# A new order table for the steps of a fused linear-attention and gated-MLP kernel

## The chip, the cores and the metric

The kernel runs on one core of a Trainium2 chip. The metric is the device time of one execution in microseconds (us). TensorE is called PE in the profile (its weight loads PEld), VectorE DVE, ScalarE ACT, GpSimd POOL and SyncE SP. Every load and store of data, but one small one that POOL issues, is issued from SP's queue.

## The reference, cut to what matters

There are 4 batches, 8 heads, 768 time steps and 48 columns per head, in float32. The first part is a gated linear recurrence with one 48 by 48 state per batch and head; its output, heads side by side, is the input x (768 by 384) of a gated MLP with a spatial mix.

```
for t in range(S):
    state = alpha[:, :, t, :, None] * state + einsum('bhd,bhe->bhde', k[:, :, t], v[:, :, t])
    y[:, :, t] = einsum('bhd,bhde->bhe', q[:, :, t], state)
...
h = maximum(x @ w_in, 0)                  # 384 -> 1024
u, v = h[..., :512], h[..., 512:]
v_n = (v - mean(v)) / sqrt(var(v) + 1e-6)
v_s = einsum('ts,bsd->btd', w_spatial, v_n) + b_spatial[None, :, None]
out = (u * v_s) @ w_out                   # 512 -> 384
```

## The kernel before

**Stages.** Time is cut into chunks of 128 steps: 6 chunks per batch, 24 in all, numbered 0 to 23. The first 8 chunks are worked in 4 *pairs* (0 to 3) of 256 steps, the others singly. The work is cut into 1156 *steps*, each bound to one engine. A step's name is used below with the number of its pair or chunk.

- Loads: `ac`, `kc`, `qc`, `vc` bring alpha, k, q and v; a pair's load is 384 KB, a chunk's 192 KB. They are numbered by chunk, so pair 1 is `ac 2` and so on. `w_in 1` and `w_in 0` are the two column halves of w_in, `w_sp 0` to `w_sp 2` thirds of w_spatial, and `w_out` the last weight. Weights land in a float32 buffer (`raw_w`, two of them) and are cast to bf16 (`cast`).
- Attention of a pair: `lnp` takes the log of alpha on ACT; `cump` sums it over time by a matmul with a triangle of ones (built on POOL by `c_tri`); `einvp` and `eexpp` take exp of minus and plus that sum (ACT); `ktp` and `qtp` scale k and q by them; `vbp` casts v; `tr k` and `tr q` transpose on PE and `ev` copies the result from PSUM; `sc` computes scores; `m` masks them (DVE); `ya` and `y` make the output from scores and from the state. `updq`, `z`, `S`, `ebcp` and `sb` update the state, scale it, and copy it for the next `y`.
- Attention of a single chunk: the same, as `ln`, `cum`, `einv`, `eexp`, `kt`, `qt`, `vb`, `trk`, `ev`, `upd`, `sc`, `m`, `y`.
- `xs` casts an output to bf16, `xt` transposes it, `xe` copies it into x transposed.
- The MLP of batch b: `v b t` is x @ w_in's second half with a ReLU; `bn`, `rs`, `vn` normalise it (mean and variance, reciprocal root, scaling); `u b f h` is the first half; `wt` and `we` transpose w_spatial; `s b d h` is the spatial matmul in two parts and an addition of the bias on DVE; `g` multiplies by u (POOL or DVE); `o b t` is the product with w_out and its copy from PSUM, and `st` the store. The last output tile is made in two half-column pieces, `oh`. `bb` and `be` spread the bias.
- `c_...` steps fill constants at the start; `c_junk` fills the operand of junk matmuls.

**Order.** Nothing is ordered while the program runs but by semaphores. The Python code first lists all steps with what each depends on, and `replay` then emits them in the order of the table `PLAN` (lines 57 to 108). A word of the table is a letter for the engine (P for PE, D for DVE, A for ACT, G for POOL, S for an issue on SP, Q for the landing, which emits nothing) and the step's number. So the table sets each engine's own sequence, and with it which of the allowed engines does a step. Each engine runs its sequence strictly as emitted. `P58:512:512:192` adds junk: before the step's first matmul, PE runs float32 matmuls of 512, 512 and 192 columns into that step's PSUM bank. PSUM's 8 banks go round in the order in which `bank()` is called, so also in the table's order.

Of the kernel before, what the change touches and what calls it, by code (L numbers as in the profile page):

```python
# [60 lines left out]
P134:512:108 P86 G121 D122 A135 P78 D87 S182 Q183 P126 D88 P124 P89 D80 S184 Q185 A186 P136 D91 A79 A127 D90 G81 A137  # L61
G123 D83 A125 G82 P149:512:500 A133 S322 Q323 P146 D151 P92 A22 D150 P96 A93 P197 D23 A97 D21 P94 D147 P187 A198 P98
A95 S24 Q25 D148 G200 A188 P100:228 A189 G190 P203 S326 Q327 A199 P138 D191 A101 D201 G84 A99 P195 D102 G8 A204 P205
G85 P193 A139 P103 D140 S324 Q325 A202 D206 G141 D196 P152 A104 D143 G142 A194 P215 S29 Q30 D105 G192 P153 A330 P157
G144 P207 D154 A106 G145 D158 P155 P331 D209 A156 D216 P341 A208 P159 G28 A332 D217 P212 A160 G210 A26 D214 P172 G211
A342 D213 P161 A333 G27 A173 D335 P218 S33 Q34 A343 A162 S328 Q329 P219 D345 P170 G334 A220 S382 Q383 D163 P223 P349
P221 A224 S384 Q385 P164 G344 D350 A222 P339 D174 A171 P225 P337 A165 P168 D340 A226 P166 D107 A175 D338 P227 A167
D176 D108 A169 P230 D32 A228 D177 P238 A231 D31 P247 S386 Q387 D35 A239 P347 D232 A248 P250 P244 A249 P242 G36 D229
A348 P236 A252 D251 P362 A233 S37 Q38 G346 D245 P253 D246 A243 G336 P240 D364 A237 S424 Q425 P351 A390 D363 A255 S428
Q429 D235 P359 A254 D234 P391 A352 D353 S388 Q389 P274 D360 A393 A241 G354 P270 A392 D356 P275 D361 A395 G394 P266  # L70
D276 P267 G357 D396 P271 A40 G39 D268 P398 D272 P259 S426 Q427 G355 A400 P365 D399 A261 D260 P256 G358 P405 S430 Q431
D366 A432 P369 P278 G269 D370 S495 Q496 P367 P433 D258 A368 P371 G273 D257 P279 S41 Q42 D407 A372 P294 A434 G397 D406
P295 A435 S461 Q462 G277 A437 D280 P376 S463 Q464 G436 P408 D296 P282 D438 A409 G439 P401 A377 P290 D402 A503 S465
Q466 P410 P440 G403 D411 P283 D412 A441 G281 D442 P373 D284 G297 P291 A374 P420 D292 S499 Q500 G285 A46 P447 D421 P443
P504 S497 Q498 A469 G43 D378 P413 A45 G404 P470 A44 S592 Q593 D449 P286 A472 A505 D448 P416 S467 Q468 A471 P287 D444
A474 D417 P418 G445 S501 Q502 A507 D288 P306 G473 A414 D508 S594 Q595 A419 P450 D415 G293 A307 P422 A451 S596 Q597
P298 D475 A423 G506 D375 S663 Q664 P477 A299 P452 G476 P302 A479 D453 D478 G289 A600 P480 P510 A303 D481 P484 S626
Q627 G446 D454 A512 P601 D511 P318 D485 G482 A602 S598 Q599 A603 A379 D486 P513 G483 P314 A605 S665 Q666 D515 G604
A319 P487 A509 D606 S628 Q629 P455 A488 D514 P608 S705 Q706 A456 D315 P489 P516 A610 D609 P310 S632 Q633 G607 D490
A517 D457 A491 P615 A671 P518 S630 Q631 P492 D519 A520 D381 A458 P521 D311 A493 D617 P530 A522 S667 Q668 D616 P528  # L80
A494 P611 D380 P534 S707 Q708 A529 D460 A634 P532 D459 D612 A523 S743 Q744 P548 G613 A531 P672 D524 P635 G641 S777
Q778 A713 P540 D533 A535 P618 A525 S709 Q710 P560 A674 A637 A636 D527 P544 D526 S669 Q670 A673 G638 P714 A639 P561
A676 S711 Q712 D640 P549 G614 A619 D677 P541 A715 S779 Q780 G675 D550 A716 P545 A751 D542 P642 S781 Q782 G551 P620
D562 P552 A622 D621 A718 S749 Q750 P553 D546 G543 A643 D719 P645 P623 A644 S745 Q746 D554 G717 A785 D646 P649 A678
P679 S747 Q748 G647 D650 P721 A624 P556 G547 A723 D651 P557 A681 D722 G563 P652 D680 S783 Q784 P682 D558 A653 P686
G555 P728 D683 S877 Q878 P654 D687 P536 A656 G684 A655 P537 D688 A720 S873 Q874 G648 P786 D729 P752 A787 P564 S907
Q908 G685 D538 A754 A758 P724 P657 D730 A753 S875 Q876 G539 A789 P565 D725 A658 D790 S990 Q991 P731 G755 A756 D566
P689 A732 P568 D757 G788 A690 D659 P759 A569 P733 S879 Q880 G726 P691 P576 D734 A692 G559 D625 A735 A760 S909 Q910
# [1071 lines left out]
```

## Time and profile before

| | |
|---|---|
| median of 3 runs | 142.24 us (142.18 to 142.88) |
| profiled execution | 142.43 us, of which the span of instructions is 140.6 us |
| granted TensorE clock, mean | 0.997 |
| busy PE / DVE / ACT / POOL | 135.3 / 118.5 / 108.1 / 83.9 us |
| DMA | 28.64 MB in 89000 packets, mean 204 GB/s |
| junk matmuls | 22 instructions, 10.7 us |

Busy time of PE has modelled ends and can overlap waits, so the gaps from start to start of its steps are read as well. A line of the timeline gives start, duration, engine, line of the code, operation and tiles; lines of helpers (`copy` is L198 on ACT and L200 elsewhere, matmuls of the MLP are all L819) are told apart by tiles. Of idle time, the brackets name what ended it.

### The profile page before, as it was taken

What the parts mean: (1) busy time and instruction counts of PE and PEld (TensorE: products, weight loads), DVE (VectorE), ACT (ScalarE), POOL (GpSimd) and SP (SyncE); (2) the same over time, 40 slices, a digit from 0 to 9 for tenths busy, and PEclk for the clock granted to TensorE, in tenths of its full rate; (3) what the DMA queues carried; (4) which work ended last, traced back from release to release, by engine and by line L of the source; (5) the groups of instructions that cost most, each with busy time, mean ns of one, the idle gap of its engine ahead of it and who ended that gap; (6) DMA issues with size and microseconds to landing.
All of it is one profiled execution on the core that took longest, in us unless ns stands there. A gap on an engine that the chain in (4) does not pass through costs nothing.

```text
span 140.6 us, 4974 instructions
## 1 busy us (share of the span) xinstructions
PE 135.3 (96%) x1921; PEld 84.1 (60%) x1921; DVE 118.5 (84%) x292; ACT 108.1 (77%) x279; POOL 83.9 (60%) x148
## 2 busy tenths in 40 slices
PE   7999999999999999999999999999999999999990
PEld 3357566574767656665665765656657666566560
DVE  7187799989999789899689999999899899987850
ACT  3487898899976678999989699989967978751021
POOL 6816458861469996970289999402788599002520
PEclk9999999999999999999999999999999999999998
DMA  4999997989999979989999998999999120005535
GB/s 101 320 324 328 338 254 245 295 286 315 267 226 161 306 145 215 203 175 210 188 199 190 188 200 171 199 200 220 257 222 225 71 107 7 0 23 212 215 146 192
DMA packets 89000, 28.64 MB, mean 204 GB/s; under 512 B 83728, under 2 KB 87440, under 8 KB 88976
## 3 DMA queue, kind: packets, MB, share of 16 engines
q1 hardware_dynamic: 88944, 28.32, 81.8%
q8 instruction: 15, 0.25, 0.7%
q14 instruction: 9, 0.07, 0.2%
q0 software_dynamic: 32, 0.00, 0.0%
HBM read 23.60 MB, written 4.72 MB: 201 GB/s over the span
## 4 chain that ended last, share of the span: by engine, by line
PE 59%; ACT 9%; DMA 9%; SPq 7%; POOL 5%; DVE 5%; issue 4%; ACTq 0%; POOLq 0%
PE bank L819 42%; SPq L432 7%; DMA raw_w<-in_moe_w_in_dram 5%; DMA ac<-in_alpha_dram 3%; PE bank L710 3%; PE bank L745 2%; PE bank L773 2%; PE bank L731 2%; PE bank L657 2%; PE bank L767 1%; POOL kt L681 1%; DMA out_dram<-raw_w 1%; PE bank L389 1%; POOL kt L474 1%; ACT vn L880 1%
## 5 line engine op out<-in xcount | busy, mean ns | idle before, releaser
L819 PE MATMUL bank<-w_spT,vn 128*128 128x384 bf16 x192 | 35.9, 326 | 0.0
L980 POOL TENSOR_TENSOR gT<-vsb,uT 128x384 bf16<-128x384 f32 x27 | 25.0, 939 | 12.5 <-DVE vsb L967 12.1
L819 PEld LDWEIGHTS <-vn 128*128 128x128 bf16 x192 | 17.3, 97 | 10.2
L681 POOL TENSOR_TENSOR kt<-kc,binv 128x384 bf16<-128x384 f32 x16 | 14.6, 917 | 11.9 <-ACT bc L676 7.3
L756 DVE TENSOR_TENSOR ptm<-bank,mask 128x512 bf16<-128x512 f32 x32 | 20.5, 680 | 0.7 <-PE bank L745 0.6
L819 PE MATMUL bank<-xT,w_in 128*128 128x384 bf16 x96 | 19.9, 326 | 0.0
L967 DVE TENSOR_TENSOR vsb<-bank,bsp_bc 128x384 f32<-128x384 f32 x31 | 16.6, 551 | 3.6 <-PE bank L819 3.0
L819 PE MATMUL bank<-w_in,xT 128*128 128x512 bf16 x72 | 18.8, 379 | 0.3 <-ACT xT L198 0.2
L819 PE MATMUL bank<-w_out_sb,gT 128*128 128x384 bf16 (+1 forms) x100 | 18.6, 320 | 0.0
L198 ACT COPY kqT<-bank 128x512 bf16<-128x512 bf16 x28 | 15.9, 598 | 2.2 <-PE bank L710 1.5
L335 POOL TENSOR_TENSOR state<-state,bc 128x192 f32<-128x192 f32 x20 | 10.1, 506 | 12.4 <-DVE mvs L896 5.5
L200 POOL CAST sbd<-state 64x192 bf16<-64x192 f32 x40 | 13.7, 341 | 2.1
L204 ACT ACTIVATE v_sb<-bank 128x512 bf16<-128x512 f32 x20 | 12.0, 602 | 2.4 <-PE bank L819 2.3
L884 DVE BATCH_NORM_STATS2 stats<-v_sb 128x6 f32<-128x512 bf16 x20 | 13.6, 682 | 0.0
L204 ACT ACTIVATE uT<-bank 128x384 bf16<-128x384 f32 x23 | 10.9, 492 | 2.2 <-PE bank L819 2.0
L819 PEld LDWEIGHTS <-w_in 128*128 128x128 bf16 x96 | 8.7, 97 | 5.9
L198 ACT COPY xT<-bank 128x192 bf16<-128x192 bf16 (+1 forms) x25 | 9.0, 377 | 4.1 <-PE bank L389 2.9
L819 PEld LDWEIGHTS <-gT 128*128 128x128 bf16 x100 | 8.8, 97 | 5.0
L188 PE MATMUL bank<-junk 128*128 128x512 f32 (+6 forms) x22 | 10.7, 613 | 1.1 <-DVE junk L1050 1.1
L585 DVE TENSOR_TENSOR ptm<-bank,mask 128x512 bf16<-128x512 f32 x16 | 10.3, 682 | 1.0 <-PE bank L574 1.0
L198 ACT CAST x_sb<-bank 128x384 bf16<-128x384 f32 x19 | 9.0, 494 | 2.3 <-PE bank L773 2.3
L916 DVE TENSOR_SCALAR vn<-v_sb,mvs,rstd 128x512 bf16<-128x512 bf16 x24 | 8.9, 404 | 1.5 <-ACT rstd L909 1.5
(129 smaller groups left out, 281.2 us busy)
## 6 DMA issues: line engine op xcount, KB each, us to landing
ac<-in_alpha_dram SPq DMA_DIRECT2D x16, 192.0 KB, 4.0
kc<-in_k_dram SPq DMA_DIRECT2D x16, 192.0 KB, 4.0
qc<-in_q_dram SPq DMA_DIRECT2D x16, 192.0 KB, 4.2
vc<-in_v_dram SPq DMA_DIRECT2D x16, 192.0 KB, 4.0
raw_w<-in_moe_w_spatial_dram SPq DMA_DIRECT2D x3, 768.0 KB, 5.5
out_dram<-raw_w SPq DMA_DIRECT2D x11, 192.0 KB, 2.9
out_dram<-o_sb SPq DMA_DIRECT2D x9, 192.0 KB, 1.9
ac<-in_alpha_dram SPq DMA_DIRECT2D x4, 384.0 KB, 4.6
```

What stands on the lines that cost most here:

```text
L188: nc.tensor.matmul(out=flat[:, 0:cols].rearrange("p (a b) -> p a b", a=4), lhsT=junk, rhs=junk[:, None, 0:n].to_broadcast([128, 4, n]), st ...
L198: nc.scalar.copy(out=out, in_=in_)
L200: ENG[eng].tensor_copy(out=out, in_=in_)
L204: nc.scalar.activation(out=out, in_=in_, func=AF.Relu)
L335: ENG[eng].tensor_tensor(out=st["state"], in0=st["state"], in1=st["bc"][:, :, None].to_broadcast([128, HP, D]), op=ALU.mult)
L585: nc.vector.tensor_tensor(out=st[f"ptm{par}"][:, s], in0=st[f"pt{s}{par}"], in1=mask2[:, par], op=ALU.mult)
L681: ENG[eng].tensor_mul(out=k_blocks(kt3)[:, :, :, 0:D], in0=quad(st["kc"]), in1=st["binv"])
L756: nc.vector.tensor_tensor(out=st["ptm"][:, s], in0=st[f"pt{s}"], in1=mask4, op=ALU.mult)
L819: return lambda ps: nc.tensor.matmul(out=out(ps), lhsT=lhsT(), rhs=rhs(), start=start, stop=stop)
L884: nc.vector.bn_stats(out=stats, in_=d["v_sb"][:, tt, :])
L967: nc.vector.tensor_tensor(out=hold["vs"], in0=ps[:, 0:TH], in1=bsp_bc[:, th, :], op=ALU.add)
L980: ENG[eng].tensor_tensor(out=bt[b]["gT"][:, dsl, cols], in0=hold["vs"], in1=bt[b]["uT"][:, dsl, cols], op=ALU.mult)
```

## The change

The table `PLAN` is replaced; nothing else. The table was made by a search that began with both pieces of w_in requested right behind the loads of the first pairs; the table that came out has them as the 10th and 15th issue of SP, which is where they were. All 1156 steps are there in both tables. 105 steps are given to another engine; DVE has 265 steps (260 before), ACT 253 (258), PE 300, POOL 115 and SP 111 in both. Junk columns are 5468 (4312 before).

The table's diff, first and last lines:

```
-D0 S49 Q50 D17 D13 S109 Q110 G47 Q48 D5 S53 Q54 G10 D7 S51 Q52 D2 D3 D11 G18 D15 D12 D1 S55 Q56 A57 G14 S111 Q112 G16
-P58:512:512:192 P264 A59 P68 A60 S113 Q114 G9 A69 D62 A70 D6 P66:512:232 S115 Q116 D71 P262 A67 D4 P74 A117 D61 S178
-Q179 D72 A263 P128:492 D75 A265 P118 D73 A129 P76 S19 Q20 P64 A130 G131 D65 A119 D77 S180 Q181 A120 G63 D132
...
+D0 S49 Q50 D1 D6 S51 Q52 G47 Q48 D12 D13 S109 Q110 D3 G14 D4 S53 Q54 D11 D5 G9 D15 D17 G18 S111 Q112 A57
+P68:512:512:192 S113 Q114 P264 A69 P262 P58 D263 A70 A59 S55 Q56 D2 A60 D61 G71 A265 S178 Q179 A117 D72 D62 G16
+P74:512:512:448 P118 S115 Q116 P76 P64 A119 P66 D77 A75 G121 D65 A120 S19 Q20 D7 D67 G10 P89:512:208 P128 S180 Q181
...
```

In names, each engine's sequence at the start. Junk columns stand in brackets ahead of their step.

```
SP   before: ac 0, ac 2, qc 0, kc 0, vc 0, kc 2, qc 2, vc 2, ac 4, w_in 1, kc 4, qc 4, vc 4, ac 6, w_in 0, qc 6, kc 6, w_sp 0, w_sp 1, vc 6, ac 8
SP   after:  ac 0, kc 0, ac 2, qc 0, kc 2, qc 2, vc 0, ac 4, vc 2, w_in 1, kc 4, qc 4, vc 4, ac 6, w_in 0, qc 6, kc 6, w_sp 0, w_sp 1, vc 6, ac 8
PE   before: [1216] cump 0 0, bb 1, cump 0 1, [744] tr q 0 0, bb 0, tr k 0 1, [492] cump 1 1, cump 1 0, tr q 0 1, tr k 0 0, [620] tr k 1 1, sc 0 0, updq 0, tr q 1 0, tr k 1 0, sc 0 1, tr q 1 1, [1012] sc 1 1, sc 1 0, ya 0, y 1, cump 2 1, xt 0, cump 2 0, xt 1, [228] v 0 0, tr k 2 1, updq 1, tr q 2 0, tr q 2 1, tr k 2 0, v 0 1, ya 1, sc 2 1, y 2, y 3, updq 2, xt 2, cump 3 0, cump 3 1, xt 3, sc 2 0, v 0 3, v 0 2, ya 2
PE   after:  [1216] cump 0 1, bb 1, bb 0, cump 0 0, [1472] tr k 0 1, cump 1 0, tr q 0 1, tr k 0 0, tr q 0 0, [720] sc 0 1, cump 1 1, [1024] tr q 1 0, updq 0, sc 0 0, tr q 1 1, tr k 1 0, tr k 1 1, [656] sc 1 0, ya 0, sc 1 1, y 1, cump 2 0, xt 1, xt 0, cump 2 1, updq 1, v 0 1, tr k 2 0, tr q 2 0, [260] tr q 2 1, v 0 0, tr k 2 1, ya 1, sc 2 0, y 2, y 3, updq 2, xt 2, xt 3, sc 2 1, cump 3 0, v 0 2, cump 3 1, v 0 3, ya 2
ACT  before: lnp 0, einvp 0 0, eexpp 0 0, einvp 0 1, eexpp 0 1, ev q 0 0, lnp 1, be 0, be 1, einvp 1 1, eexpp 1 1, einvp 1 0, eexpp 1 0, ev k 1 1, lnp 2, ebcp 0, ev q 1 0, ev q 1 1, ev k 1 0, vbp 1 1, cast w_in 1 1, xs 0, xs 1
ACT  after:  lnp 0, einvp 0 1, eexpp 0 1, einvp 0 0, eexpp 0 0, be 1, lnp 1, einvp 1 0, ev k 0 1, eexpp 1 0, einvp 1 1, eexpp 1 1, ebcp 0, lnp 2, ev k 1 0, ev q 1 1, cast w_in 1 0, cast w_in 1 2, cast w_in 1 1, xs 1
DVE  before: ... vbp 0 1, ev k 0 0, ev q 0 1, qtp 1 1, qtp 1 0, m 0 0 0, m 0 0 1, z 0, m 0 1 1, m 0 1 0, z 1, m 1 1 1, m 1 1 0, cast w_in 1 2, cast w_in 1 0, m 1 0 0, m 1 0 1, qtp 2 0, qtp 2 1, bn 0 0, z 2, ev q 2 1, ev q 2 0, z 3, bn 0 1, xs 2, xs 3, z 4, m 2 1 0, m 2 1 1, m 2 0 1, m 2 0 0
DVE  after:  ... ev k 0 0, c_col, ev q 0 0, m 0 1 1, m 0 1 0, qtp 1 0, ktp 1 1, qtp 1 1, ev q 1 0, z 0, m 0 0 1, m 0 0 0, ev k 1 1, z 1, m 1 0 1, xs 0, m 1 0 0, m 1 1 0, m 1 1 1, qtp 2 0, z 2, qtp 2 1, ev k 2 0, z 3, ev q 2 1, bn 0 1, ev k 2 1, bn 0 0, m 2 0 1, z 4, m 2 0 0, m 2 1 1, m 2 1 0
POOL before: b_sp, c_m4, c_m2 1, c_tri, c_m2 0, c_id, ktp 1 1, vbp 0 0, ktp 1 0, S 0, vbp 1 0, sb 0, ...
POOL after:  b_sp, c_tri, c_id, c_m2 1, ktp 0 1, c_m2 0, ktp 1 0, c_m4, vbp 0 0, vbp 0 1, vbp 1 0, vbp 1 1, S 0, sb 0, ...
```

Further on, three casts of w_spatial go from DVE to POOL (`cast w_sp 0 0`, `0 1`, `1 0`) and one from POOL to ACT. `vbp 3 1` goes from POOL to DVE. Ahead of SP's last load stand two stores (six before). The end of PE's sequence:

```
before: ... s 3 2 1 (second part), s 3 3 1 (second part), s 3 1 1 (both parts), o 3 0, o 3 2, o 3 1, oh 0, o 3 4, o 3 3, oh 1
after:  ... s 3 1 1 (both parts), s 3 3 1 (second part), o 2 5, o 3 2, o 3 0, o 3 3, oh 0, o 3 1, o 3 4, oh 1
```

More of the change, by code (lines that the diff above doesn't have):

```diff
@@ L63 @@
[L63 to L87, printed above, removed]
@@ new lines @@
+Q502 A479 G446 P480 A478 D303 P298 G506 S705 Q706 A307 D481 P283 D508 A600 G289 S598 Q599 A299 P510 D284 P484 A511
+P450 G482 D485 P601 A512 G285 P422 D486 A451 S663 Q664 P513 A603 A602 P452 G483 P487 D454 A605 S707 Q708 D514 P310
+G604 A453 A488 D606 P455 A423 S628 Q629 D515 A379 P489 P608 A311 D509 S626 Q627 P314 D609 A610 D491 P516 A456 D490
+S632 Q633 D607 P492 D380 A315 D457 A517 S669 Q670 P615 A493 P518 P318 D381 A458 D519 D520 A713 P611 D459 P521 A319
+D616 S709 Q710 A494 P532 D617 A522 S630 Q631 P530 D460 P534 A523 D533 S665 Q666 P618 A671 D612 P528 D524 A634 G613
@@ new lines @@
+P548 S777 Q778 D619 A525 G614 P635 D535 A531 P620 S667 Q668 P560 A641 D527 D621 P714 A637 A636 D526 S779 Q780 P540
+A715 G638 P549 A622 S745 Q746 A716 A529 P561 D550 G717 A639 P645 S711 Q712 A718 P541 D640 G551 P672 D562 S743 Q744
+P642 A674 A673 D646 P544 D542 A644 G647 P545 S781 Q782 D643 A676 G675 P552 D719 A678 S907 Q908 D677 P553 G648 D546
+P649 S747 Q748 P721 G563 D554 P679 P682 D650 A681 P623 G547 A722 D651 P536 A624 S873 Q874 D683 G543 P652 D680 A723
+P537 D625 S749 Q750 A653 G684 P686 A785 P728 D538 G685 P654 S948 Q949 P564 A655 D656 D687 A751 G720 P786 P657 S783
@@ L109 @@
+G1120 P1136 A870 P1128 S871 Q872 A1137 P1140 S1138 Q1139 D1129 P1148 S1130 Q1131 A1141 P1132 D1149 S1142 Q1143 P1144
+S1150 Q1151 D1133 P1152 S1134 Q1135 A1145 A1153 S1146 Q1147 S1154 Q1155
 """
```

59 lines of the change are left out of this document (36 added, 23 removed).

## The prediction

> **What bounds the kernel now.** I read the page's head first, then the timeline of the first 20 us, the landings of the DMA issues, the busy time by stretches, and the timeline of the end.
>
> ```profile
> span 140.6 us, 4974 instructions
> PE 135.3 (96%) x1921; PEld 84.1 (60%) x1921; DVE 118.5 (84%) x292; ACT 108.1 (77%) x279; POOL 83.9 (60%) x148
> ...
> PE   7999999999999999999999999999999999999990
> ...
> DMA  4999997989999979989999998999999120005535
> ...
> PE 59%; ACT 9%; DMA 9%; SPq 7%; POOL 5%; DVE 5%; issue 4%; ACTq 0%; POOLq 0%
> ```
>
> TensorE is busy in every slice, and the chain that ended last lies on it for 59%. The order of PE's own work cannot make that work shorter, so a new order can only change the time in which PE waits. The DMA engines are full up to 105 us and then empty. Where PE waits shows first in the start:
>
> ```profile
> 4.28 0.84 ACT L443 ACTIVATE la<-ac 128x768 bf16<-128x768 f32 x1 [2.26 <-DMA ac<-in_alpha_dram]
> ...
> 5.41 0.14 POOL L273 MEMSET lt_pair<- 64x64 bf16 x1
> ...
> 11.09 1.28 PE L188 MATMUL bank<-junk 128*128 128x512 f32 x4
> ...
> 14.08 0.84 ACT L443 ACTIVATE la<-ac 128x768 bf16<-128x768 f32 x1 [0.86 <-PE bank L502]
> ...
> 17.19 0.62 ACT L198 CAST w_in<-raw_w 128x512 bf16<-128x512 f32 x1 [0.34 <-DMA raw_w<-in_moe_w_in_dram]
> ```
>
> The columns are start, duration, engine, line, operation and, in brackets, idle time and what ended it. Up to 20 us PE is filled with junk matmuls while the first chain log, cumsum, exp, transposes, scores and masks runs. The landings of the DMA issues go by place in SP's queue and not by name: 4.25, 5.46, 6.67, 7.89, 9.08, 10.39, 11.61, 12.80, 13.99 us, then 17.17 for the first piece of w_in. That is 1.21 us for each 384 KB and 3.18 for a piece of w_in.
>
> **The change, part by part.** All 1156 steps stay. 105 of them change engine; DVE gets five more, ACT five fewer. Both pieces of w_in keep their places in SP's queue (10th and 15th), and the queue's places 10 to 21 are the same loads, so w_in lands at 17.17 and 26.09 as before; "right behind the first pairs' loads" is only where the search began. What changes are the loads ahead, the junk, and the engines' orders.
>
> *Start, to the 45th PE step* (`ya` of pair 2, behind the same 44 steps in both tables). Before, it starts at 28.42, just behind the last mask on DVE (27.53 to 28.21). In the new order:
> - The first log still waits for 4.25. `c_tri` now runs first on POOL (1.21 us from about 2.0) and is no longer the last to come (5.55 before); first exp 6.07 against 6.15: -0.1.
> - ACT does four exps and one bias copy (about 0.5 each) to 8.7, then the log of pair 1 to 9.5 (alpha lands at 6.67). PE has 1472 junk columns ahead of `tr k 0 1`. The 744 columns at 6.95 took 1.25 us, 1.68 ns a column, so these end at about 9.43, as that log does. The cover is full. Without it, the 1156 extra junk columns of the table would cost 1.94 us.
> - k of pair 0 lands 2.4 us sooner, q 1.2 later (7.89), needed at 8.3. The first scores start at 11.8 (12.53 before).
> - Then it loses: 1024 junk columns end at 14.2, `updq 0` comes at 14.4 (12.88 before). ACT has `ebcp 0` ahead of the log of pair 2, so that log starts at 15.4 instead of 14.08, though its alpha lands at 12.80. Behind it stand the two copies that `sc 1 0` needs (0.5 each); `sc 1 0` starts at 17.3, `y 1` at 18.4 against 17.73: +0.7.
> - From 17.8 DVE works through 8 masks (0.61 from start to start: 4.9), one `xs` (0.47), 2 `qtp` (1.0), 3 `ev` (1.0), 3 `z` (0.8), 2 `bn` (1.7), and waits 0.5, mostly for one exp: 10.4, so the last mask ends at 28.3 and `ya` starts then. Before, the same stretch ran from 17.12 and held besides two casts of w_in (0.7), two `xs` in place of one and two `ev` in place of three. These moves to ACT give the 0.7 back: -0.1.
>
> *To 42 us.* The same count brings both tables to their 65th step (again the same set) at 36.2 against 36.6. Then `updq 3` waits 0.4 for a copy of v that is now on DVE, behind `we` and `vn`: even. I take 0 for all up to 42 us; each of some ten hand-overs may be off by 0.1 to 0.2, so bounds of -0.6 and +0.7.
>
> In this stretch three casts of w_spatial go from DVE to POOL. The rows:
>
> ```profile
> 34.66 1.08 POOL L200 CAST w_row<-raw_w 128x768 bf16<-128x768 f32 x1 [3.92 <-PE bank L831]
> ...
> 41.83 0.82 POOL L200 CAST w_row<-raw_w 128x768 bf16<-128x768 f32 x1
> ...
> 34.05 1.01 DVE L200 CAST w_row<-raw_w 128x768 bf16<-128x768 f32 x2
> ```
>
> The cast beside DVE's own casts took 1.08 us, the other 0.82. Three at 1.08 behind `c_ut` (done 32.05) end at 33.1, 34.2, 35.3; PE wants them at 34.0, 34.2, 35.6. So at the dearer row they cost 0.1 at most. [...]
>
> *Middle, 42 to 118 us.*
>
> ```profile
> 62.00:72.00 10.00, 9.98 (x123) 6.14 (x121) 7.94 (x24) 9.77 (x31) 2.86 (x6) 1.00 0.97 190
> 72.00:82.00 10.00, 9.86 (x163) 6.43 (x162) 9.71 (x23) 8.39 (x23) 9.60 (x16) 1.00 1.00 195
> 82.00:92.00 10.00, 9.92 (x176) 6.03 (x174) 9.41 (x24) 9.90 (x28) 7.43 (x13) 1.00 0.97 190
> 92.00:102.00 10.00, 10.00 (x96) 6.11 (x95) 8.92 (x25) 9.26 (x28) 3.55 (x5) 1.00 0.95 226
> ```
>
> Columns: stretch, length, busy PE, weight loads, DVE, ACT, POOL, clock, DMA, GB/s. DVE idles 4.0 of these 40 us, ACT 2.7. I summed each table's steps by the rows' durations: between PE steps 120 and 220 (59 to 102 us) the new table gives DVE 1.8 us more and ACT 2.8 less. PE's start-to-start gaps beyond the usual one of such a step sum to 2.8 us from 60 to 95. They are 0.92 in 72 to 82 (DVE fullest) and 0.79 in 82 to 92 (ACT fullest): a full DVE costs 0.13 more per 10 us, 0.5 over 40, and I take half, +0.3, since only part of the load moves. Bounds: -1.4 (half of the 2.8 goes with ACT's load) and +1.8 (DVE's addition whole). Of the distances in PE work between a step and what it feeds, none of the new table from step 45 on is shorter than the rows of the chain between (before: two, by 0.07), so no single join costs anything by itself. Loads land 2 to 5 us ahead of use here; the new queue has two stores instead of six ahead of the last load (0.9 us each), so the last ones come 3 to 4 us sooner, which nobody waits for: 0.
>
> *End.*
>
> ```profile
> 133.27 4.07 PE L819 MATMUL bank<-w_out_sb,gT 128*128 128x384 bf16 x28
> ...
> 134.25 0.91 POOL L980 TENSOR_TENSOR gT<-vsb,uT 128x384 bf16<-128x384 f32 x1 [1.60 <-DVE vsb L967]
> ...
> 137.98 0.41 SPq L1011 DMA_DIRECT2D out_dram<-raw_w  x1
> ```
>
> The last POOL product needs 0.56 + 0.91 and hand-overs, 1.8 us, behind its spatial group; the new table puts 0.49 + 3 x 0.65 = 2.4 us of PE work there: 0. Were that cover gone, 0.9 would be late. The last half output, its copy and store are the same: 0.
>
> Sum: 0 + 0.3 + 0 on the profiled execution's 142.43 (span 140.6 and 1.83 around) is 142.7; the median of the runs shown is 0.19 lower: 142.5.
>
> **The rivals.**
> - *Slower: the start's loss is kept.* Place: `y 1`, +0.7 at 18.4 us. For it: the log of pair 2 stands behind `ebcp 0`. Against it: DVE has 1.1 us less to do behind. It decides if DVE waits over 1 us between 17.8 and 28.3, above all for the exps of pair 2. Price 0.7 beside the middle's 0.3: 143.2.
> [...]
> - *Slower: DVE is the bound of the middle.* Its added 1.8 us are paid whole: 144.0. It decides once DVE is over 97% busy in 62 to 102.
> - *Faster: ACT was the bound of the middle.* The chain of before lies on ACT from 62.55 to 67.6 and from 86.14 to 91.1 us. Half of the gaps gone, 1.4: 140.8; with a start 0.3 better or worse 140.5 to 141.2.
>
> **How the numbers follow.** A measurement tells 0.5% (0.7 us) from no change. Forecast (within 141.5 to 142.95) 0.33, the likeliest single case; start kept 0.16, POOL casts 0.08, DVE bound 0.16, together slower 0.40; ACT relieved 0.27. The forecast's own range is 141.8 to 143.2 by the start's bounds. For 8 in 10 the range takes in the slow cases to 144.2 and half of the fast one, from 141.0.
>
> **What would show it.** Right: first scores near 11.8, `y 1` near 18.4, the mask that ends DVE's row near 28.3 and `ya` behind it; w_in landing at 17.2; DVE about 1.7 us busier, ACT 2.3 less. Wrong: `ya` of pair 2 over 0.6 us from 28.3; POOL's w_row casts over 1.2 us with PE idle behind them; a middle whose PE gaps move by over 0.7; stores that end the span other than by the last half output.

## The result and the profile after

The changed kernel takes 144.66 us (median of six runs, 144.3 to 145.37) against 142.21 (142.07 to 142.88): ratio 1.0164, 95% interval 1.0129 to 1.0199. It is slower by 1.6%, outside the predicted range. Ratios here leave out executions over 1.5% above the fastest of their kernel; medians and ranges hold all.

The head of the page of the changed kernel, and its chain by engine (its own time is 144.97 us, 1.77 around the span):

```profile
span 143.2 us, 4984 instructions
PE 136.6 (95%) x1927; PEld 85.6 (60%) x1927; DVE 119.5 (83%) x297; ACT 107.0 (75%) x274; POOL 84.4 (59%) x148
...
PE   7999989979999999999999999999999999999990
...
PEclk9999999999999999999999999999999999999998
DMA  4999988999899989989699798989989013092055
...
PE 68%; DMA 11%; SPq 7%; ACT 4%; DVE 3%; issue 2%; POOL 2%; ACTq 0%; POOLq 0%; DVEq 0%
```

The span grew by 2.6 us, PE's busy time by 1.3. At 1.67 ns a column from start to start, junk sums to 9.1 us (5468 columns) against 7.2 (4312): 1.9 more. That sum is not what the junk costs, since part of it lies in time in which PE would have waited anyway. PE's row now has an 8 at 18 to 21 us and a 7 at 29 to 32. DVE is 1.0 us busier and ACT 1.1 less.

The start in the timeline of the changed kernel (start, duration, engine, line, operation, idle time and what ended it):

```profile
2.99 0.14 POOL L273 MEMSET lt_pair<- 64x64 bf16 x1
...
4.24 0.84 ACT L443 ACTIVATE la<-ac 128x768 bf16<-128x768 f32 x1 [2.23 <-DMA ac<-in_alpha_dram]
...
10.19 1.43 PE L188 MATMUL bank<-junk 128*128 128x512 f32 x4
...
15.16 0.83 ACT L443 ACTIVATE la<-ac 128x768 bf16<-128x768 f32 x1
...
17.59 1.66 ACT L198 CAST w_in<-raw_w 128x512 bf16<-128x512 f32 x3 [0.56 <-DMA raw_w<-in_moe_w_in_dram]
```

`c_tri` is out of the way at 3.0, the log of pair 2 starts 1.08 later than before, and w_in lands 0.4 later. What PE waits for from 0 to 42 us (us in total, times, longest), first the changed kernel, then the kernel before:

```profile
PE bank L502 <- POOL kt L474: 1.1, 1, 1.1
PE bank L188 <- DVE junk L1050: 1.1, 1, 1.1
PE bank L365 <- ACT x_sb L198: 0.6, 1, 0.6
```

```profile
PE bank L188 <- DVE junk L1050: 1.1, 1, 1.1
PE bank L819 <- ACT xT L198: 0.2, 1, 0.2
PE bank L831 <- DVE w_row L200: 0.2, 1, 0.2
PE bank L574 <- DVE state L330: 0.2, 1, 0.2
```

The new wait of 1.1 us, with the load that it hangs on, in the timeline of the changed kernel:

```profile
31.37 1.78 POOL L474 TENSOR_TENSOR kt<-kc,binvp 128x384 bf16<-128x384 f32 x2 [1.48 <-DMA kc<-in_k_dram]
...
32.33 0.40 PE L502 MATMUL bank<-ident,kt 128*128 128x128 bf16 x4 [1.08 <-POOL kt L474]
...
33.61 2.37 POOL L200 CAST w_row<-raw_w 128x768 bf16<-128x768 f32 x3
```

k of pair 3 landed at 31.23 us (28.47 before). The last line is the three casts of w_spatial: 0.82 us each.

Behind 42 us, the stretches of the changed kernel (stretch, length, busy PE, weight loads, DVE, ACT, POOL, clock, DMA, GB/s), and what PE waits for in 42 to 118 (the same view of the kernel before lists no wait):

```profile
62.00:72.00 10.00, 9.73 (x127) 5.84 (x125) 9.73 (x28) 9.68 (x30) 2.60 (x6) 1.00 0.91 178
72.00:82.00 10.00, 10.00 (x157) 6.47 (x156) 8.97 (x22) 8.04 (x23) 8.93 (x14) 1.00 0.95 187
82.00:92.00 10.00, 9.99 (x159) 6.43 (x158) 9.23 (x21) 8.73 (x27) 8.98 (x15) 1.00 0.97 190
92.00:102.00 10.00, 9.98 (x116) 5.96 (x114) 9.56 (x28) 9.34 (x29) 2.32 (x5) 1.00 0.98 194
```

```profile
PE bank L710 <- POOL kt L681: 0.3, 1, 0.3
PE bank L389 <- DVE x_sb L200: 0.2, 1, 0.2
```

Both waits are between 59 and 72 us. In the first stretch DVE and ACT are both at 97%, and PE's busy time is the lowest.

Where the time goes is read best at PE steps behind which both tables have done the same set. The table gives the end of that step less its end in the trace of before (14.96, 29.00, 36.72, 74.82 and 137.35 us), for the two traces of the new table and those of the experiments. "Rate doubles" is the time in us at which the trace's record of the granted clock begins; there the start-to-start distance of equal matmuls halves (a 512-column junk matmul: 854 to 429 ns). Before that moment the trace holds no record of the clock, and the page's row stands at 9 there too, so the row does not show the first doubling.

| kernel | rate doubles | 17th | 45th | 65th | 156th | last |
|---|---|---|---|---|---|---|
| after | 5.4 | +1.18 | +0.59 | +1.69 | +2.31 | +2.54 |
| after_again | 6.4 | +1.66 | +1.18 | +1.28 | +1.90 | +2.07 |
| head_new | 10.3 | +3.53 | +2.61 | +2.70 | +3.25 | +3.27 |
| tail_new | 4.8 | -0.38 | -0.38 | -0.37 | +1.08 | +1.34 |
| no_junk | 24.1 | +3.72 | +3.61 | +3.71 | +4.32 | +4.50 |
| kc6_first | 5.2 | +1.11 | +0.19 | +0.29 | +0.90 | +1.36 |
| sc_junk_cut | 4.7 | +0.46 | +0.88 | +0.98 | +1.59 | +1.77 |
| k_junk_half | 6.3 | +1.41 | +1.64 | +1.73 | +2.35 | +2.53 |
| mid_mended | 4.4 | +0.81 | +3.00 | +2.82 | +3.52 | +3.69 |
| all_mended | 10.3 | +1.86 | +0.95 | +1.05 | +1.74 | +2.19 |
| tail_mended | 4.5 | -0.30 | -0.06 | -0.05 | +1.15 | +1.31 |
| before_cut | 5.2 | -0.11 | +0.02 | +0.03 | +0.02 | +0.03 |
| after_filled | 6.7 | +2.69 | +2.54 | +2.63 | +3.26 | +3.71 |
| new_filled | 4.1 | +1.03 | +0.12 | +0.22 | +0.84 | +1.02 |
| before_filled | 5.0 | -0.04 | +1.57 | +1.42 | +1.41 | +1.42 |

### The profile page after: what moved, and what is told of

Read it like the earlier page. It is cut to its first block, busy times and chain, and to the rows that moved or that the text cites. A ratio compares the mean times of both kernels' runs of the same rounds, so it can differ in the third digit from the quotient of the medians.

```text
span 143.2 us, 4984 instructions
## 1 busy us (share of the span) xinstructions
PE 136.6 (95%) x1927; PEld 85.6 (60%) x1927; DVE 119.5 (83%) x297; ACT 107.0 (75%) x274; POOL 84.4 (59%) x148
## 4 chain that ended last, share of the span: by engine, by line
PE 68%; DMA 11%; SPq 7%; ACT 4%; DVE 3%; issue 2%; POOL 2%; ACTq 0%; POOLq 0%; DVEq 0%
PE bank L819 48%; SPq L432 7%; DMA kc<-in_k_dram 7%; DMA raw_w<-in_moe_w_in_dram 5%; PE bank L745 3%; PE bank L710 3%; PE bank L773 2%; PE bank L657 2%; PE bank L767 2%; PE bank L389 2%; PE bank L731 2%; PE bank L831 1%; POOL sbd L200 1%; DVE ptm L756 1%; ACT w_in L198 1%
## 5 line engine op out<-in xcount | busy, mean ns | idle before, releaser
L819 PE MATMUL bank<-w_spT,vn 128*128 128x384 bf16 x192 | 35.8, 326 | 0.0
L980 POOL TENSOR_TENSOR gT<-vsb,uT 128x384 bf16<-128x384 f32 x26 | 24.1, 939 | 13.4 <-DVE vsb L967 13.2
L819 PEld LDWEIGHTS <-vn 128*128 128x128 bf16 x192 | 17.3, 97 | 10.8
L335 POOL TENSOR_TENSOR state<-state,bc 128x192 f32<-128x192 f32 x20 | 10.3, 513 | 22.4 <-DVE state L328 6.5
L819 PE MATMUL bank<-xT,w_in 128*128 128x384 bf16 x96 | 18.7, 326 | 0.0
L198 ACT COPY kqT<-bank 128x512 bf16<-128x512 bf16 x26 | 14.6, 593 | 2.4 <-PE bank L710 2.3
L188 PE MATMUL bank<-junk 128*128 128x512 f32 (+6 forms) x28 | 12.8, 586 | 1.1 <-DVE junk L1050 1.1
L585 DVE TENSOR_TENSOR ptm<-bank,mask 128x512 bf16<-128x512 f32 x16 | 10.3, 680 | 1.4 <-PE bank L574 1.4
L200 DVE COPY kqT<-bank 128x512 bf16<-128x512 bf16 x22 | 8.7, 413 | 2.4 <-PE bank L502 2.4
L204 ACT ACTIVATE uT<-bank 128x384 bf16<-128x384 f32 x21 | 10.1, 495 | 0.1
L198 ACT COPY xT<-bank 128x192 bf16<-128x192 bf16 (+1 forms) x23 | 8.0, 379 | 2.5 <-PE bank L365 1.1
```

Source lines behind the costliest of these rows:

```text
L188: nc.tensor.matmul(out=flat[:, 0:cols].rearrange("p (a b) -> p a b", a=4), lhsT=junk, rhs=junk[:, None, 0:n].to_broadcast([128, 4, n]), st ...
L198: nc.scalar.copy(out=out, in_=in_)
L200: ENG[eng].tensor_copy(out=out, in_=in_)
L204: nc.scalar.activation(out=out, in_=in_, func=AF.Relu)
L335: ENG[eng].tensor_tensor(out=st["state"], in0=st["state"], in1=st["bc"][:, :, None].to_broadcast([128, HP, D]), op=ALU.mult)
L585: nc.vector.tensor_tensor(out=st[f"ptm{par}"][:, s], in0=st[f"pt{s}{par}"], in1=mask2[:, par], op=ALU.mult)
```

## The experiments

**Which part loses: head_new and tail_new.** The new order to PE's 65th step with the old order behind it, and the reverse.

```
head_new: new table to PE's 65th step, then the remaining steps in the old order
tail_new: old table to PE's 65th step, then the remaining steps in the new order
```

> The new table up to PE's 65th step (the same set of PE steps in both tables), then the rest in the old table's order and with its engines. In the two traces step 65 is left 1.6 us later by the new table, of the 2.5 us in all. Theory of the start (late k of pair 3, junk): +1.6 us on before, 143.8. Theory of the middle (DVE's added load): at most +0.4, 142.6, since the middle is the old one.

Measured: 145.0 us (144.27 to 145.75), ratio 1.0171 (1.0110 to 1.0233).

> The old table up to PE's 65th step, then the rest in the new table's order. Theory of the start: +0.9 us at most, 142.6 to 143.1. Theory of the middle: +1.8 or more, 144.0.

Measured: 143.89 us (143.76 to 143.98), ratio 1.0108 (1.0080 to 1.0136).

The new order of the start alone makes it slower by about as much as the whole change. The new rest costs by itself too, so neither "start" nor "middle" is the whole of it. The two do not add up to the change, for two reasons in the table. Each splice has a seam (0.55 us behind the 65th step in head_new, 0.63 in tail_new). And the trace of head_new is one in which the rate doubles late (10.3 us). Behind its seam head_new keeps +3.25 to +3.27 to the end: the old order of the rest loses nothing. From the 65th step to the end the new order loses 0.85 and 0.79 us in the two traces of the whole change, 1.07 in kc6_first and 1.71 less the seam, 1.08, in tail_new.

**Is junk what the start pays: no_junk.**

```
-P74:512:512:448  P89:512:208  P126:512:512  P146:512:144  P205:260  P347:120
+P74              P89          P126          P146          P205      P347
```

> The new table with all junk matmuls but the first 1216 columns left out (4252 columns, 7.1 us at 1.67 ns each). If junk is paid for on PE (it ends later than what it covers for), the start gets shorter by the part that lies bare, 0.6 to 1.9 us: 142.8 to 144.0. If k of pair 3, landing at 31.2 us, is what holds PE at 32.3 us, taking junk away ahead of it gains nothing: 144.4 to 144.7. If the junk keeps the clock up, the granted clock falls in the first 20 us and it gets slower than 144.7.

Measured: 146.21 us (146.16 to 146.93), ratio 1.0283 (1.0247 to 1.0320). It is slower than the change by 1.55 us. Without junk the rate doubles only at 24.1 us, and the useful matmuls of the start run at half rate. So this start needs junk; the question is how much of it, and where.

**Late k of pair 3: kc6_first.** Its load is issued ahead of `w_in 0`, the second of the two pieces of w_in in the queue. (The expectations of all_mended and kc6_sc_cut call it the first; the edit is the same there.)

```
-... A188 S24 Q25 ... S324 Q325 ...
+... A188 S324 S24 Q25 ... Q325 ...
```

> The new table with one word moved: the load of k of pair 3 is requested ahead of the second piece of w_in instead of two places behind it. Theory of the late load: k lands near 25 us instead of 31.2, the POOL product of pair 3 starts with its exp at about 30.3 and the transposes 1.0 us sooner: 143.6, less what the later piece of w_in (near 28.5) costs the u groups (they start at 29.9; its casts are wanted by then: 0 to 0.5). Theory of junk: 144.6, no change.

Measured: 143.91 us (143.65 to 144.41), ratio 1.0114 (1.0079 to 1.0149), 0.75 less than the change. k of pair 3 lands at 22.69, and PE does not wait. This looked like proof, but after_again, below, takes the reason away: in that second trace of the unchanged table the load landed at 26.97 and nothing waited for it. The late landing belongs to the first trace. Why this kernel is still the better one is not settled. It is better by more than the noise of the table itself, whose two medians, here and in after_again, are 144.66 and 145.06.

**Four at once: sc_junk_cut, k_junk_half, mid_mended, all_mended.**

```
sc_junk_cut: -P89:512:208        +P89
k_junk_half: -P74:512:512:448    +P74:512:232
mid_mended:  GpSimd  -404 446 506  +404 506 446     (kt 11 ahead of sb 9)
             ScalarE -671 634      +634 671         (ln 13 ahead of ln 14)
             VectorE -524 619      +619 524         (xs 12 ahead of mv 1 4)
all_mended:  the three above and kc6_first
```

> The new table without the 720 filler columns ahead of the first score step (sc 0 1) and nothing else changed. Theory 'exposed filler': in the trace after, the last copy that this step needs ends at 10.71 and the step starts at 11.54, behind filler that began at 10.19; VectorE's first masks wait for these scores (gap of 1.38 us to 12.08) and it is busy from there to 17.1, so the step and the masks come about 0.75 us earlier and 0.5 to 0.8 us of it reaches the end: 143.9 to 144.2 us against 144.66. Rival 'the loads decide': the masks come earlier, but VectorE then waits longer for q of pair 2 (landing 21.22) and TensorE for k of pair 3 (31.23), and the end stays at 144.5 to 144.8. Rival 'filler keeps the clock up': the clock falls back and the time is over 145.5, as without all filler (146.21).

Measured: 144.27 us (143.29 to 145.68), ratio 1.0102 (1.0059 to 1.0145): 0.39 less than the change, and no more than the 0.40 between the two medians of the unchanged table. PE's 17th step comes 0.72 us earlier than in the trace after, and the 25th 1.05. Of this the edit gives 0.45: `tr k 0 1`, ahead of it, is 0.27 earlier already, since the rate doubled 0.7 us sooner, and 0.33 comes from w_in, which landed at 15.96 instead of 17.57. The 720 columns were bare for 0.74 us: the last copy ended at 10.71, `sc 0 1` started at 11.54. Then PE stood inside `updq 2`, with its inputs ready. The timeline of sc_junk_cut:

```profile
24.56 0.44 PE L543 MATMUL bank<-vbp,kt 64*128 64x48 bf16 x11
26.18 0.29 PE L543 MATMUL bank<-vbp,kt 64*128 64x48 bf16 x5 [1.17 <-issue]
```

> The new table with 744 filler columns ahead of its first transposes (tr k 0 1) instead of 1472, which is the number that the old table has ahead of its own; nothing else changed. Theory 'filler at half clock': the granted rate rises at another moment in each run (5.4 us in the profile after, 10.5 in that of the new table to step 65 only, where these 1472 columns took 3.9 us instead of 2.5 and their end lay 1.7 us past the copy that they cover, against 0.1 us where the clock was up). So the fastest runs stay as they are (144.3) and the slowest (145.4) come down by 0.7 to 1.5: median 144.0 to 144.4, spread smaller. Rival 'cover is full': the copies end at 8.74, the transposes cannot start sooner, and nothing changes: 144.5 to 144.8. Rival 'filler raises the clock': with fewer columns the clock rises later and the median is over 145.

Measured: 144.91 us (144.33 to 147.21), ratio 1.0171 (1.0129 to 1.0213): no gain. With the rate doubled in time the transposes wait for GpSimd's k at 9.19 instead of behind junk. This kernel too stood inside `updq 2`, for 1.0 us. Two other executions, 145.97 and 147.21 us, have a mean granted clock of 0.987 and 0.986 where the rest have 0.997 to 1.000; the next experiment shows what that means.

> The new table with three moves of one step each: on GpSimd kt 11 ahead of sb 9, on ScalarE ln 13 ahead of ln 14, on VectorE xs 12 ahead of mv 1 4. Theory 'three waits': TensorE's waits for these three steps (0.36 us at 59.6, 0.16 at 70.6, 0.31 at 71.2, the same to 0.01 in three runs with this order) are the whole loss between its 65th and 156th step, so the time falls by 0.6 to 0.8: 143.9 to 144.1 us. Rival 'an engine bounds the middle': what was moved back now makes TensorE wait instead (for sb 9, ln 14 or rs 1 4), and the time stays within 0.3 of 144.66.

Measured: 145.8 us (144.38 to 146.4), ratio 1.0209 (1.0158 to 1.0260): a miss. From the 65th to the 156th step it loses 0.70 us, as before the moves (0.62). The three waits are gone, but PE now waits for `kt 12` (0.21), for the bank of `u 1 1 1` and for `kt 13` (0.12): the rival of the expectation. And it stood 1.35 us inside `updq 2`, after which PE's rate was halved again, from 28.33 to 31.75 us, where the trace records a granted clock of 0.50. Here the page's row does show it, as the 6 in its ninth slice:

```profile
PEclk9999999969999999999999999999999999999999
```

The mean granted clock of this execution is 0.988. A second of the six, 146.4 us, has 0.987, and the others have 0.997 to 1.000, so part of the miss is this and not the moves. The timeline of mid_mended, then, for the duration of the same two matmuls, that of after_again:

```profile
24.91 0.34 PE L543 MATMUL bank<-vbp,kt 64*128 64x48 bf16 x7
26.61 0.40 PE L543 MATMUL bank<-vbp,kt 64*128 64x48 bf16 x9 [1.35 <-issue]
...
28.34 1.06 PE L818 MATMUL bank<-w_in,xT 128*128 128x512 bf16 x2
```

```profile
26.37 0.39 PE L543 MATMUL bank<-vbp,kt 64*128 64x48 bf16 x9 [0.27 <-issue]
...
28.11 0.59 PE L818 MATMUL bank<-w_in,xT 128*128 128x512 bf16 x2
```

> The new table with all of it: k of pair 3 requested ahead of the first piece of w_in, no filler ahead of sc 0 1, 744 columns instead of 1472 ahead of tr k 0 1, and the three moves in the middle. If the named causes are the whole loss and add up (0.75 measured for k of pair 3, 0.5 to 0.8, 0 to 0.6, 0.6 to 0.8), 142.0 to 142.6 us, level with the kernel before (142.21). If they overlap, because the first load or engine mended uncovers the next, 143.0 to 143.6.

Measured: 143.62 us (143.13 to 144.75), ratio 1.0095 (1.0057 to 1.0133): 1.04 less than the change, and not level with the kernel before. The edits overlap, and the middle's did nothing.

**What the stop in `updq 2` is.** It lies behind PE's 350th matmul of the record in sc_junk_cut, k_junk_half, mid_mended and after_again, though the first two have four and two junk matmuls fewer ahead of that step. (A few records are missing in these traces, so the count is good to one or two.) In the trace of the DMA packets, queue q8, which the page calls "instruction", brings blocks of 16384 bytes. The second such packet ended at 24.74, 25.43, 25.01 and 24.99 us in sc_junk_cut, k_junk_half, mid_mended and after_again, and PE went on at 26.18, 26.88, 26.61 and 26.37: 1.38 to 1.60 us later each time. The two filled kernels below that stop there, after_filled (0.60 us) and before_filled (0.67), go on 1.22 and 1.43 us behind the packet. PE did not stop where it came to the place later than that, by 1.5 us or more: in before at 25.04 with the packet's end at 22.65, in after at 25.76 and 23.96, in kc6_first at 25.40 and 23.24, in head_new at 27.82 and 25.54. No wait in the record explains the stop, and its place goes by the count of matmuls, not by the step. That PE waits there for its own program is the author's reading of the queue's name and of these times, and is not shown: no run moved the packet alone. What makes the block late is open. The packet started within 0.3 us of PE's 230th weight load in before (20.81 and 20.53) and tail_new, and 1.1 to 4.1 us behind it in the traces with the new start; but three later traces with the old start have 1.3 to 2.9. In kc6_first, all_mended and new_filled, which ask for k of pair 3 first, it ended at 23.1 to 23.3 and PE did not stop. That may be the gain of kc6_first; no run tests it.

**Both starts' edits together, the same table again, the middle once more, and the old table's junk: kc6_sc_cut, after_again, tail_mended, before_cut.**

```
kc6_sc_cut:  kc6_first and sc_junk_cut
after_again: no edit
tail_mended: tail_new, the moves of mid_mended, and
             GpSimd  -483 604 +604 483 (kt 12 ahead of sb 10)
             ScalarE -525 531 +531 525 (u 1 1 1 ahead of rs 1 4), einv 13 ahead of vb 13
before_cut:  old table, -P149:512:500 +P149:512:140
```

> The new table with two changes in its start: k of pair 3 requested ahead of the first piece of w_in, and no filler ahead of sc 0 1. The theory 'start lost to exposed filler and to late transfers' holds that the first gave 0.75 and that the second brings TensorE 0.72 us ahead at its 17th step, but that this gain was lost again in three of the four runs since, where TensorE stood 1.0 to 1.4 us inside updq 2 for no data at all: its second block of program (a 16384-byte packet) ended at 24.7 to 25.4 us, and TensorE went on 1.44 to 1.6 us after that. Both runs with k of pair 3 first had that packet in by 23.1 to 23.2. So here it stands nowhere, and both gains add: 143.0 to 143.3 us, TensorE's 45th step within 0.3 us of the kernel before. If the gains share one cover, or the block of program is late again, 143.7 to 144.3.

Measured: 145.09 us (143.36 to 146.53), ratio 1.0094 (1.0065 to 1.0124). Three runs lie at 143.36 to 144.07, the lowest near the expectation; the other three lie at 146.12 to 146.53, and the trace is of one of these, so no step is read from it. One thing that can split the runs of a kernel shows in two other traces with a late doubling, head_new (1472 columns) first, all_mended (744) second:

```profile
7.41 4.07 PE L187 MATMUL bank<-junk 128*128 128x512 f32 x6
11.32 0.39 PE L501 MATMUL bank<-ident,kt 128*128 128x128 bf16 x4
```

```profile
7.41 2.69 PE L187 MATMUL bank<-junk 128*128 128x512 f32 x4
9.88 0.60 PE L501 MATMUL bank<-ident,kt 128*128 128x128 bf16 x4
```

GpSimd's k was ready at 9.51 in both. At half rate 1472 columns are bare for 1.7 us, 744 for 0.3. The run of head_new with this trace took 145.67 us, its two lowest 144.27 and 144.33: 1.4 less, near the 1.6 more that these columns are bare than in the trace after. That the two lowest had an early doubling is not shown, since one execution of each kernel is traced. For all_mended these distances are 0.9 to 1.5 us (144.62 traced, 143.13 to 143.74 the five lowest), more than its 0.3 bare; the rest may be the half rate of its useful matmuls.

> The new table unchanged, for a second trace. If what differs from run to run is when the clock of TensorE rises (4.5 to 10.5 us so far) and when the second block of program comes (packet end 23.0 to 25.5), this trace shows other values of both than the first (5.4 and 24.0), and the time follows them: near 144.3 where both are early, 145.0 to 145.5 where one is late. If the start is the same in every run of a program, it repeats 29.6 for the 45th step and 31.2 for k of pair 3.

Measured: 145.06 us (144.49 to 145.66, four runs; the traced one is the fastest), ratio 1.0189 (1.0152 to 1.0225). Doubling at 6.4 us instead of 5.4, second block at 24.99 instead of 23.96: the start does differ from run to run, as the first theory of this expectation had it. The time did not follow as numbered, since this trace had no late k.

> The old table to TensorE's 65th step, then the new order (143.89 when run before, with a spread of 0.2) with six moves of one step: kt 11 ahead of sb 9 and kt 12 ahead of sb 10 on GpSimd; ln 13 ahead of ln 14, u 1 1 1 ahead of rs 1 4 and einv 13 ahead of vb 13 on ScalarE; xs 12 ahead of mv 1 4 on VectorE. With the first three moves alone, kt 11, ln 13 and xs 12 no longer held TensorE, but kt 12 (0.28), cum 15 (0.37, for the bank that u 1 1 1 empties) and kt 13 (0.18) held it as long. Theory 'a few steps out of place': now 0.5 to 0.8 of it comes out: 143.1 to 143.4 us. Rival 'the other engines bound the middle of the new order': GpSimd has no pause from 57 to 63 us, the wait moves on again, and the time stays at 143.7 to 144.0.

Measured: 143.64 us (143.48 to 144.06), ratio 1.0092 (1.0071 to 1.0112). 0.25 us against tail_new, less than expected from the six moves. What PE waits for in 42 to 118 us, first tail_new, then tail_mended:

```profile
PE bank L818 <- issue: 0.3, 2, 0.2
PE bank L709 <- POOL kt L680: 0.2, 1, 0.2
PE bank L388 <- DVE x_sb L199: 0.2, 1, 0.2
```

```profile
PE bank L818 <- DVE vn L915: 0.5, 1, 0.5
PE bank L818 <- issue: 0.3, 2, 0.2
```

The waits moved on to `vn` and gathered there: 0.5 us at 71 us. It is no step out of place: from 62 to 72 us ACT is busy for 9.79 of the 10 us in tail_mended and DVE for 9.06, and what one move gave another took.

> The old table with 652 filler columns ahead of sc 1 1 instead of 1012, nothing else. In the trace before, the copy that this step needs ends at 15.95 and filler holds it to 16.65; VectorE's next masks wait for it (0.81 us, to 17.12). Theory 'exposed filler costs the start': 0.3 to 0.6 us come out, 141.6 to 141.9 us against 142.2, faster than both kernels. Rival 'the loads decide': w_in (17.17) and q of pair 2 (20.17) come next on ScalarE and VectorE, and the time stays within 0.2 of 142.2. Rival 'the clock falls back without it': over 142.5.

Measured: 141.97 us (141.81 to 142.91, twelve runs) against 142.34 (17 runs), ratio 0.9981 (0.9963 to 0.9998). This is the one version faster than both kernels, by 0.2%, with an interval that just leaves out no change. The traced execution took 142.47 us, no less than that of before (142.43), so it shows one in which the gain is lost. The masks and q of pair 2, before:

```profile
17.12 1.29 DVE L585 TENSOR_TENSOR ptm<-bank,mask 128x512 bf16<-128x512 f32 x2 [0.81 <-PE bank L574]
...
20.39 1.02 DVE L481 TENSOR_TENSOR qt<-qc,bank 128x384 bf16<-128x384 f32 x2
```

And in before_cut:

```profile
16.53 1.29 DVE L584 TENSOR_TENSOR ptm<-bank,mask 128x512 bf16<-128x512 f32 x2 [0.33 <-PE bank L573]
17.33 0.62 ACT L197 CAST w_in<-raw_w 128x512 bf16<-128x512 f32 x1 [0.42 <-DMA raw_w<-in_moe_w_in_dram]
...
20.41 1.02 DVE L480 TENSOR_TENSOR qt<-qc,bank 128x384 bf16<-128x384 f32 x2 [0.73 <-ACT bank L468]
```

The masks come 0.59 us earlier, but q of pair 2 is scaled at 20.41, as before. ACT first has the cast of w_in, at 17.33 behind its landing, and the exps stand behind. That is the rival "the loads decide" in this trace; the seven runs of the twelve at 141.8 to 142.0 keep some of the gain, and no trace shows how.

**Does filling PE's pauses fix when the rate doubles: after_filled, new_filled, before_filled.** An entry of 64 columns in each pause (every junk entry stands in the trace as two matmuls: 22 for the 11 entries of before). "Window" in the expectations is the guess that a late doubling comes from these pauses, so that with them filled no run has one; "chance" is that filling them changes nothing. No run so far shows that the pauses matter.

```
after_filled:  P264 +:64   P262 +:64   P58 +:64
new_filled:    the same, and kc6_first, sc_junk_cut, k_junk_half
before_filled: before_cut, P264 +:64, P68 +:64
```

> The new table with 128 filler columns (an entry of 64) ahead of each of bb 1, bb 0 and cump 0 0, where TensorE stands 0.1 to 0.2 us each between 5.9 and 6.8 us; nothing else. So far the rate of TensorE doubled at 4.5 to 6.7 us in ten traces and at 10.3 to 10.6 in three, never between, and in the three the filler ahead of tr k 0 1 took 2.5 us for 744 columns or 3.9 for 1472. [...] Then no run of this kernel is in the upper group (145.3 to 145.7 for the new table): all within 144.2 to 144.8, median 144.4 to 144.6. Rival 'the moment is chance': one run in three stays at 145.3 to 145.7. [...]

Measured: 145.44 us (145.38 to 146.16), ratio 1.0209 (1.0177 to 1.0241).

> The new table with k of pair 3 first, no filler ahead of sc 0 1, 744 instead of 1472 filler columns ahead of tr k 0 1, and the three pauses filled with 128 columns each. With the same start and the pauses unfilled, runs fell into two groups (143.1 to 143.7 and 144.4 to 144.8, three of eight), and the trace of one of the upper group had the rate doubled at 10.3 us. Theory 'window': one group, 143.1 to 143.8. Rival 'chance': a third of the runs at 144.4 or above. If both parts of the start are mended and only the middle's 0.8 to 1.1 us is left, 143.1 to 143.4.

Measured: 143.8 us (143.35 to 144.41), ratio 1.0097 (1.0062 to 1.0133).

> The old table with 652 instead of 1012 filler columns ahead of sc 1 1 (141.97 when run so, eight of twelve runs at 141.8 to 142.0, four at 142.4 to 142.9), and 128 filler columns ahead of bb 1 and of cump 0 1, in the two pauses of TensorE between 5.9 and 6.5 us. Theory 'window': the runs at 142.4 and above vanish, median 141.8 to 142.0, faster than both kernels by 0.2% or more. Rival 'chance': a third of the runs stay at 142.4 or above.

Measured: 142.54 us (141.96 to 144.26, twelve runs), ratio 1.0011 (0.9982 to 1.0040).

Inconclusive, and the numbers are a miss. Runs did not fall into one group. The fillings are themselves bare: 1.1 us in all in after_filled, where four of six runs lie within 0.1 us, but 1 us higher. All three traces have the doubling by 7 us, which three traces cannot prove. The trace of before_filled has the stop inside `updq 2` too (0.67 us, block at 23.86, PE on at 25.29), and afterwards the half rate, from 25.48 to 28.90 us: the old table can be struck as well. The row of its page, with a 5 in the eighth slice:

```profile
PEclk9999999599999999999999999999999999999999
```

The trace's record of the granted clock says more about the moment of doubling. All of its stretches but the last of each trace last a whole number of times 3.413 us: 39 times in before (133.12 us), 40 in after (136.53), 36 in no_junk (122.88), and 7, 1 and 33 in mid_mended. So in these traces the rate changes only at points that lie a whole number of times 3.413 us apart, and where they lie differs between executions. Of the 16 traces used, 13 have such a point at 4.1 to 6.8 us, and the rate doubles there. In head_new, all_mended and no_junk, reckoned back from the doubling in steps of 3.413 us (an estimate: 10.30 and 10.33 less 3.41, 24.05 less five times that), the point fell at 6.9 to 7.0, and the rate stayed at half. The first two doubled at the next point, and no_junk five points later. So in these traces the late doublings go with a point that falls later than 6.8 us, 1.5 us behind the end of the first 1216 columns at 5.3 us. That the short pauses behind those columns are the reason is not shown: the points of the three filled traces are at 4.1, 5.0 and 6.7 us, so the filling was not tried where it would have mattered. With the first columns from 1.05 us on, the doubling came anywhere from 4.1 to 10.3 us, and at 24.1 in no_junk.

## Why the prediction was wrong, point by point

The step that failed is the start's term, "I take 0 for all up to 42 us". The runs show 1.28 and 1.69 us there instead. The middle's term had the right sign and was too small: +0.3, where 0.8 was measured.

- **First chain.** Right to a few tenths. First scores 11.8 predicted, 11.54 and 12.03 in the two traces of the new table; `updq 0` 14.4, 14.17 and 14.65; `sc 1 0` 17.3 and `y 1` 18.4, 17.23 and 18.44 in the first.
- **"The cover is full."** This failed too, for all junk but the place that I looked at. I priced the junk as a sum (1.94 us without cover) and set it to nothing, from one place, the 1472 columns, at full rate. The price of the 720 columns ahead of `sc 0 1` was not looked at: they are 0.74 us bare in both traces, and DVE's masks wait for them. And the 1472 are covered only while the rate doubles in time: bare for 0.1 us in both traces of the new table, 1.7 in head_new. Before, the worst bare stretch is 0.60 us, at `sc 1 1`, and before_cut shows that little of it counts. In the new table it counts for more: without the 720 columns the distance from `tr k 0 1` to `sc 0 1` is 0.24 to 0.45 us shorter (all_mended, new_filled, sc_junk_cut), and PE's next steps keep this.
- **"These moves to ACT give the 0.7 back", `ya` at 28.3.** The last mask ended at 28.44 in the first trace, as predicted. But `ya` started at 29.01, since the new order has PE in `v 0 3` until then (28.27 to 29.08); I had looked at DVE alone. In after_again the stop behind the 350th matmul came on top, and `ya` started at 29.61.
- **"0 for all up to 42 us", bounds -0.6 and +0.7.** Measured at the 65th step: +1.69 and +1.28. This term is the main error. In the first trace 1.1 of it is k of pair 3, which I had landing by its place in the queue. w_in at "17.17 as before" came at 17.57, and at 15.9 to 16.3 in most later traces; k of pair 3, in the same place, landed at 26.2 to 31.2. The place fixes the first to no better than 1.7 us and the second to no better than 5. (142.5 with these bounds is 141.9 to 143.2, not from 141.8.)
- **Casts on POOL.** Right: 0.82 us each, and PE not held. DVE was busy for 2.33 of these 2.37 us, though with other work than the casts that ran beside the 1.08. No run shows the slow case by these casts to which the forecast gives 0.08.
- **Middle, +0.3.** Right in direction, mis-sized: 0.85 and 0.79 from the 65th step to the end, 0.62 of it up to the 156th in both. The loads of DVE and ACT moved as summed in kind (62 to 102 us: DVE 36.0 to 37.5, ACT 37.3 to 35.8; predicted +1.8 and -2.8 over 59 to 102). My "no single join costs anything" was read from PE's distance to its feeders alone. Over the whole span DVE is 1.0 us busier and ACT 1.1 less, where 1.7 and 2.3 were predicted. PE stands at three joins, `kt 11`, `ln 13` and `xs 12`, but they are not the cause by themselves: with these steps moved ahead PE stands at others, and the stretch costs the same (0.70 in mid_mended). That the load of the other engines is the cause fits this and is argued, not tested.
- **End, 0.** The last seven steps lose nothing, as predicted; the 0.4 us ahead of them, between the 228th and the 293rd step, are not explained.
- **Rivals.** "The start's loss is kept" had the place and the sign, at less than half of the price. It expected the exps of pair 2 to be late; shown are bare junk, and in some traces the stop in `updq 2` and a late load. "DVE bound of the middle" (144.0) came nearest in time, for a wrong reason: DVE's 1.5 us are not paid whole.

How the lateness at the 65th step adds up in the two traces of the new table, each term read at the step where it arises:

| | after | after_again |
|---|---|---|
| 17th step | +1.18 | +1.66 |
| 17th to 45th step, as in the traces without a stop or a late load | -0.92 | -0.92 |
| longer wait for `xs 1`, behind w_in (landed at 17.57 and 16.32) | +0.33 | 0 |
| stop in `updq 2` | 0 | +0.44 |
| 45th to 65th step | +0.10 | +0.10 |
| wait for k of pair 3 (landed at 31.23 and 26.97) | +1.00 | 0 |
| 65th step | +1.69 | +1.28 |

The 0.92 is that of kc6_first and head_new (0.91 in all_mended and new_filled). In four traces a stop cost about 0.17 us more than its idle time: 0.27, 0.60, 0.97 and 1.17 idle cost 0.44, 0.77, 1.15 and 1.34. The lateness at the 17th step goes with the doubling: with the junk unedited it is 0.81 at 4.4 us, 1.11 at 5.2, 1.66 at 6.4 and 3.53 at 10.3. The trace of before doubled at 6.8; tail_new has the same start, doubled at 4.8 and is 0.38 ahead of it to the 65th step. So at equal doubling (4.8), without a stop or a late load, the new start is by an estimate from these rows 0.96 + 0.38 - 0.92 + 0.10, about 0.5 us late.

So of about 2.45 us, 0.8 to 1.1 lie behind the 65th step in every trace of the new rest. The remaining 1.6 lie in the start, and vary: with the new start unedited the 65th step is 1.28 to 2.82 us late (after_again, after, head_new, mid_mended), in kc6_first and new_filled 0.2 to 0.3. About 0.5 is the new start itself, with its bare junk. The rest is a late load, a late doubling, or the stop in `updq 2` with or without half rate behind it, each in some traces only. None of the ten executions of the new table is under 144.3 us, 2.2 above the lowest of before; which of these each of them met is not known, since two are traced.

## What to carry to other kernels

Price filler matmuls at both rates of PE, and against the moment at which the step behind them gets its data: 1472 columns were bare for 0.1 us where the rate doubled at 5.4 us (after) and for 1.7 where it doubled at 10.3 (head_new). A start that was tuned on one trace holds no longer than that trace's landings (k of pair 3 at 31.23 and 26.97 us in two traces of one table); look at a second trace of the same kernel before a late load is called a cause. Where several engines were full at once, moving single steps ahead moved the wait on (0.70 us lost from the 65th to the 156th step in mid_mended, 0.62 without the moves), so judge a new order by the sum over the stretch.

## What the hardware showed that was not expected

- In six traces PE stopped behind about the 350th matmul for 0.27 to 1.35 us with no wait in the record, each time until 1.2 to 1.6 us after a 16384-byte packet of the queue "instruction", with 1.7 MB moving beside it at 342 GB/s (22 to 27 us of sc_junk_cut). That it waits for its program there is the author's reading; no run tests it.
- After two such stops (mid_mended, before_filled) PE's rate was halved for 3.41 us; the stop and the half rate together cost 2.2 us between the 33rd and 44th step of mid_mended. A stop of 1.17 us in sc_junk_cut was not followed by it; what decides stays open.
- In the 16 traces the rate changed only at points a whole number of times 3.413 us apart, and these lie elsewhere in each execution of one program: 5.4 and 6.4 us in the two traces of the new table. The page's row shows a later fall of the clock (the 6 in the ninth slice of mid_mended), but not the first rise (it stands at 9 from the start in after, where the rate doubled at 5.4 us).
